# Attention pieces placed in the order of M1 by the planner, and the last bank copied by one instruction

## The chip, the cores and the metric

One Trainium2 chip, one of its cores. The metric is the device time of one execution in microseconds; lower is better. A core has TensorE (PE, with PEld for its weight loads), VectorE (DVE), ScalarE (ACT), GpSimd (POOL) and SyncE (SP), which work at the same time and wait for each other by semaphores. Each takes its own instructions strictly in the order in which the program lists them.

## What is computed

A recurrent attention with a decay (a retention layer), and then a two-layer network with GELU on its output. Per head h the decay is gamma = 1 - 2^(-5-h); inputs q, k, v have shape (4, 8, 768, 64):

```
for t in range(S):
    state = gamma * state + outer(k[t], v[t])
    y[t] = (1 / sqrt(64)) * q[t] @ state
x = y as (batch * 768, 512)
out = gelu_tanh(x @ w_in) @ w_out        # w_in 512x2048, w_out 2048x512
```

The output is 3072 x 512 in float32.

## The kernel before

**Chunks.** The 768 steps are cut into 6 chunks of 128, numbered 0 to 5. A chunk holds 128 steps of all four batches, 512 rows of x. Each chunk passes through three stages.

*Attention of chunk c* consists of TensorE pieces, which the code names and which a line of the profile tells apart: T (L205, 8 transposes that turn q and k of one batch), A (L214, scores of one batch, 16 matmuls of 64x64), yc (L233, what the state gives to y), yi (L245, what the chunk's own scores give to y, 8 matmuls for a batch), and S (L256, the new state; not for the last chunk). Around them stand loads (SP), casts or scalings (ACT, POOL, DVE: L153, L155, L170), the copy of T's output (evT), the multiplication of A's output by a mask on DVE (ev_A1, L265), the write of y as x (ev_Y1, L272), and the update of the state (ev_S2, L277). For chunks 2 to 5 four sums over x follow on POOL (sumx), since M1 needs them.

*M1 of chunk c* is x @ w_in and GELU. For chunk 1 it is 16 plain units of 8 matmuls (L351). For chunks 2 to 5 it is done by a scheme that replaces eight block products by seven with sums of blocks: 4 groups of 7 products (PROD), each of 4 matmuls 128x128x256 (L486). A product adds into one of three banks of PSUM (X, Y, Z); between products the bank is copied out on ACT (snap), added to on DVE (add, L388), and GELU follows on ACT (L367). Products 2 to 6 of a group each need such an eviction of an earlier one; product 0 and 1 need x alone, and the third product of a group, like later ones, needs sums of x.

*M2 of chunk c* is the second layer, for chunk 0 in 16 plain units (L509), and for chunks 1 to 5 in 14 units of 8 matmuls (L498, two for each of the seven products). It needs all of M1 of that chunk and sums over g (sumg, sume on POOL or DVE). The last M2 has nothing beside it.

**What sets the order.** Chunk 0 is written out by hand. For all after it, the code at the end of the function is a planner that runs while the program is built. It holds threads of units for TensorE (thread 0: attention, threads 1 and 2: M1, thread 3: M2) and a list of operations for the other engines, with a cost for each kind (KIND), and buffers and eight PSUM banks as slots. Step by step it finds which engine can start something soonest, and writes that instruction next. A unit of TensorE is taken from the front of a thread; `unit_at` says when its inputs (`needs`) are there, and when the banks that it allocates are free. What is written is a fixed program; the planner's times are its own figures.

Each unit carries a place, the first entry of its tuple. M1 of chunk c has places c + k/28 (chunk 1: c + k/16), M2 of chunk c has c + 1.15 + u/14, and plain M2 of chunk 0 has 0.5 to 0.875. Attention of chunk c is cut into 7 units (chunk 1: 8): T, T, A of batches 0 and 1, T, T, then a unit that takes six banks (yc for two batches, A for two batches, yi for two batches), then yc, yi for the other two batches and S. In the kernel before, these units have places c - 0.9 + 0.01 i. Among the front units that are certain to be ready (`sure`, within 0.03 us), the planner takes attention first whatever its place, and else the one with the lowest place:

```
            h = min(ok, key=lambda h: (h[1] != 0, h[2][0]))
```

And where an attention unit has its inputs but waits for banks, units of M1 that would open a new X bank are held off (`held_off`).

**The last bank.** For the last chunk M2 evicts each bank of 128x256 by itself. The last one of all (product 6, second half of the rows) is copied half by VectorE (L1049) and half by ScalarE (L1050), and then a store on SP (L519) sends it out. Other copies of the kind "snap" go through `copy_on` (L153 on ScalarE).

In the texts below M1(c) is M1 of chunk c, and likewise M2(c). Where the code is reached through a helper, the line is the helper's: L153 is a copy on ScalarE, L388 any tensor_tensor of sums and additions.

Of the kernel before, what the change touches and what calls it, by code (L numbers as in the profile page):

```python
# [16 lines left out]
def kernel(  # L17
# [9 lines left out]
    nc = tc.nc  # L27
# [70 lines left out]
    def load1(eng, nm, c, b):  # L98
# [24 lines left out]
        out=misc[:, 0:1], in_=zero[:, 0:1], func=AF.Gelu_apprx_tanh, scale=1.0  # L123
# [14 lines left out]
    for j in range(2):  # L138
        for hp in range(NHP):
            nc.vector.tensor_scalar(  # L140
                out=mask[:, j, hp],
# [9 lines left out]
    def copy_on(eng, out, in_):  # L151
        if eng is nc.scalar:
            eng.copy(out=out, in_=in_)  # L153
        else:
            eng.tensor_copy(out=out, in_=in_)  # L155
# [46 lines left out]
    def mm_T(c, b, ps):  # L202
        for i, nm in enumerate("qk"):
            for hp in range(NHP):
                nc.tensor.transpose(  # L205
                    out=ps[:, i, hp], in_=pair(h16[nm, c, b], hp), identity=iden
                )
# [56 lines left out]
    def ev_A1(eng, c, b, j, ps):  # L264
        eng.tensor_tensor(out=a_sb[c, b, j], in0=ps, in1=mask[:, j], op=ALU.mult)  # L265
# [115 lines left out]
    hw = d_model // 2  # L381
# [250 lines left out]
    tok, T = {}, {}  # L632
# [17 lines left out]
    def op(*a, **k):  # L650
        todo.append(Op(*a, **k))
# [99 lines left out]
    def att(c):  # L751
        units = []

        def T1(b):
            def emit():
                mm_T(c, b, T["bank", "T", c, b])

            def ev(eng):
                qkT[c, b] = T["qkT", c, b]
                copy_on(eng, qkT[c, b], T["bank", "T", c, b])  # L760

            op("evT", ev, [("T", c, b)], [("qkT", c, b)], alloc=[(("qkT", c, b), 1)],
               free=[("bank", "T", c, b)], slack=0.5)
            return [sub(0.46, emit, [("q16", c, b), ("k16", c, b)], [("T", c, b)],
                        [(("bank", "T", c, b), 1, (128, 2, NHP, 128), F16)],
                        [("qk16", c, b)])]

        def A(b, cost):
            def emit():
                mm_A(c, b, [T["bank", "A", c, b, j] for j in range(2)])  # L770

            for j in range(2):
                r = j ^ b % 2

                def ev(eng, j=j, r=r):
                    a_sb[c, b, j] = T["a", c, b, j]
                    ev_A1(eng, c, b, j, T["bank", "A", c, b, r])

                op("evA", ev, [("A", c, b)], [("a", c, b, j)], alloc=[(("a", c, b, j), 1)],
                   free=[("bank", "A", c, b, r)], slack=1.0)  # L780
            return sub(cost, emit, [("qkT", c, b)], [("A", c, b)],
                       [(("bank", "A", c, b, j), 1) for j in range(2)])

        def yc(bs):
            def emit():
                mm_yc(c, bs, {b: T["bank", "Y", c, b] for b in bs})

            return sub(0.33, emit, [("st", c - 1, b % 2) for b in bs] + [("m1done", c - 2)],
                       [], [(("bank", "Y", c, b), 1) for b in bs], [("qkT", c, b) for b in bs])

        def yi(b, cost):
            def emit():
                mm_yi(c, b, T["bank", "Y", c, b])

            def ev(eng):
                if c not in xT:
                    xT[c] = T["x", c]
                ev_Y1(eng, c, b, T["bank", "Y", c, b])

            op("evY1" if c < 2 else "evY", ev, [("Y", c, b)] + ([("al", "x", c)] if b else []),  # L800
               [("x", c, b)], alloc=[] if b else [(("x", c), 1)],
               early=[] if b else [("al", "x", c)], free=[("bank", "Y", c, b)], slack=0.7)
            return sub(cost, emit, [("a", c, b, j) for j in range(2)] + [("v16", c, b)],
                       [("Y", c, b)], [], [("a", c, b, j) for j in range(2)] + [("v16", c, b)])

        def S(par):
            def emit():
                t = T["bank", "S", c, par]
                for i in range(2):
                    mm_s(c, 2 * i + par, t[:, i])  # L810

            def ev(eng):
                ev_S2(eng, par, T["bank", "S", c, par])

            op("evS", ev, [("S", c, par)], [("st", c, par)], free=[("bank", "S", c, par)], slack=1.5)
            bs = (par, par + 2)
            return sub(0.23, emit, [("k16", c, b) for b in bs] + [("v16", c, b) for b in bs],
                       [("S", c, par)], [(("bank", "S", c, par), 1, (128, 2, NHP, 64))],
                       [(nm, c, b) for b in bs for nm in ("qk16", "v16")])

        units += [T1(0), T1(1)]
        units.append([A(0, 0.35), A(1, 0.33)])
        units += [T1(2), T1(3)]
        if c == 1:
            units += [[yc((0, 1)), yi(0, 0.33), yi(1, 0.33)], [A(2, 0.35), A(3, 0.33)]]
        else:
            units.append([yc((0, 1)), A(2, 0.23), A(3, 0.23), yi(0, 0.33), yi(1, 0.33)])
        units.append([yc((2, 3)), yi(2, 0.33), yi(3, 0.33)] + ([] if c + 1 == NCk else [S(0), S(1)]))
        for j in (1, 3, 2, 4) if c > 1 else ():
            def emit(eng, j=j):  # L830
                xs[c] = T["xs", c]
                sum_of(eng, j, RHS, x_of4(c))

            need = {1: [("x", c, b) for b in range(B)], 3: [("x", c, b) for b in range(B)],
                    2: [("xs", c, 1)], 4: [("xs", c, 2)]}[j]
            op("sumx", emit, need + ([] if j == 1 else [("al", "xs", c)]), [("xs", c, j)],
               alloc=[(("xs", c), 1)] if j == 1 else [], early=[("al", "xs", c)] if j == 1 else [],
               slack=0.6)
        return [(c - 0.9 + 0.01 * i, u, True) for i, u in enumerate(units)]

    def m1_raw(c):
        units = []
# [138 lines left out]
    def m2_w(c):  # L981
        units, last = [], c == NCk - 1
        O = [("o0", c), ("o1", c)]
        for n, (k, lk, rk) in enumerate(PROD):
            for a in range(2):
                key = ("bank", k, c, "m2", a if last else 0)
# [31 lines left out]
                ot = O[at[0]]  # L1018
# [8 lines left out]
                if n in SNAP:  # L1027
                    alloc = [(ot, 1 if not last else 9)] if n in (0, 3) and (not last or a == 0) else []

                    def ev(eng, part=part, ot=ot, bank_of=bank_of):  # L1030
                        copy_on(eng, part(T[ot]), bank_of())

                    op("snap", ev, [did] + ([("al", ot)] if last and a else []), [("ev2", c, n, aa)],
                       alloc=alloc, early=[("al", ot)] if alloc else [], free=[key], slack=0.0)
                elif n in ADD:
                    def ev(eng, part=part, ot=ot, bank_of=bank_of):
                        tt(eng, part(T[ot]), bank_of(), part(T[ot]), ALU.add)

                    op("add", ev, [did, ("ev2", c, SNAP_OF[at], aa)], [("ev2", c, n, aa)],
                       free=[key], slack=0.0)  # L1040
                elif not (last and a == 1):
                    def ev(eng, part=part, ot=ot, bank_of=bank_of):
                        copy_on(eng, part(T[ot]), bank_of())

                    op("snap", ev, [did], [("ev2", c, n, aa)], free=[key], slack=0.2)
                else:
                    def ev(eng, ot=ot, key=key):
                        t, p = T[ot][:, 1], T[key]
                        nc.vector.tensor_copy(out=t[:, 0:hw // 2], in_=p[:, 0:hw // 2])  # L1049
                        nc.scalar.copy(out=t[:, hw // 2:hw], in_=p[:, hw // 2:hw])  # L1050

                    op("snap", ev, [did], [("ev2", c, n, aa)], free=[key], slack=0.2)
                if not last and n > 4:
                    p = n - 5
# [106 lines left out]
    while waiting or any(threads):  # L1161
        best = {}
        fronts, held_off = [], False
        for i, th in enumerate(threads):
# [4 lines left out]
                continue  # L1169
            s = max(need, free_at["PE"], r if r is not None else 1e9)  # L1170
            fronts.append([s, i, th[0], need, r])
        if fronts and fronts[0][1] == 0:
            s, _, _, need, r = fronts[0]
            if need < free_at["PE"] + 0.5 and s > max(need, free_at["PE"]):
                held_off = True
# [3 lines left out]
        fronts = [h for h in fronts if h[0] < 1e8]  # L1179
# [18 lines left out]
        if e == "PE":  # L1198
            sure = min(h[5] for h in fronts)
            ok = [h for h in fronts if h[5] <= sure + 0.03]  # L1200
            h = min(ok, key=lambda h: (h[1] != 0, h[2][0]))
            start_unit(threads[h[1]].pop(0), h[0])
        else:
            ok = [x for x in cand[e] if x[0] <= best[e] + 0.02]
            s, _, o = min(ok, key=lambda x: x[1])
            waiting.remove(o)
            finish_op(o, e, s)
# [30 lines left out]
```

## Time and profile before

| what | value |
|---|---|
| median of 3 runs | 207.44 us (207.22 to 208.33) |
| the profiled execution, its own time | 207.19 us |
| its span, from the first to the last instruction | 205.3 us |
| instructions in the trace | 5809 |
| granted TensorE clock | 1.00 |
| moved by DMA | 30.11 MB |
| last matmul starts | 201.5 us |

A row of TensorE's timeline has its start, its busy time, line, operation, what it writes and reads with shapes, and the count of merged instructions; in brackets stands the idle time before it and what ended that. Matmuls overlap their neighbours by the time in which one still drains, so the distance from one row's start to the next says more than the busy time. Rows of groups have: total busy us, mean ns of one, idle time before them, and what ended it. A row of a window has start:end, length, then busy us of PE, PEld, DVE, ACT and POOL with counts, the granted clock, the DMA share and GB/s.

### The profile page before, as it was taken

The numbers are of one execution on the slowest core, as the hardware profiler recorded it, in microseconds if no ns is written. First come the engines' busy times: TensorE is split into PE (matmuls) and PEld (weight loads), VectorE is DVE, ScalarE is ACT, GpSimd is POOL, SyncE is SP. The second block draws the span as 40 slices with busy tenths as digits, with TensorE's granted clock in tenths as the row PEclk, the third lists the DMA queues.
The fourth block names the chain that finished last, engine by engine and source line by source line (L and its number), as shares of the span: only waits on it lengthen the run. The fifth ranks groups of instructions, "written<-read, shape, count | busy, mean of one in ns | idle before, by whom it ended". The sixth has DMA issues, their size and how long they took to land. (4 is left out here: it accounts for less than half of the span.)

```text
span 205.3 us, 5809 instructions
## 1 busy us (share of the span) xinstructions
PE 196.2 (96%) x2424; PEld 156.6 (76%) x2424; DVE 147.6 (72%) x284; ACT 124.4 (61%) x223; POOL 87.8 (43%) x90
## 2 busy tenths in 40 slices
PE   7869999999999998999999999999999999999993
PEld 2346744455898887788888879888888888888882
DVE  3335585749868999997998899989656864476421
ACT  2482466054689566476599749965856577765311
POOL 0587000030222973936999957982441520024000
PEclk9999999999999999999999999999999999999999
DMA  7999999999998998976799500023000140002204
GB/s 165 287 260 206 209 204 220 219 224 240 247 209 258 255 217 194 264 173 140 231 220 249 126 3 3 0 83 129 0 0 3 42 158 8 0 5 102 102 29 179
DMA packets 83034, 30.11 MB, mean 147 GB/s; under 512 B 75456, under 2 KB 79936, under 8 KB 83008
## 3 DMA queue, kind: packets, MB, share of 16 engines
q1 hardware_dynamic: 72256, 23.45, 45.6%
q0 software_dynamic: 4224, 4.19, 12.3%
q10 hardware_dynamic: 6528, 2.10, 4.1%
q8 instruction: 19, 0.31, 0.6%
q14 instruction: 7, 0.06, 0.1%
HBM read 27.64 MB, written 6.29 MB: 165 GB/s over the span
## 5 line engine op out<-in xcount | busy, mean ns | idle before, releaser
L388 DVE TENSOR_TENSOR st<-ps,st 128x512 f32<-128x512 f32 x48 | 31.7, 683 | 10.1 <-PE ps L486 8.9
L367 ACT ACTIVATE g<-st 128x512 f16<-128x512 f32 x48 | 29.4, 633 | 14.4 <-DVE st L388 14.0
L153 ACT COPY st<-ps 128x512 f32<-128x512 f32 x48 | 27.2, 590 | 11.6 <-PE ps L486 11.4
L498 PEld LDWEIGHTS <-s_g 128*128 128x128 f16 x320 | 31.1, 98 | 3.6
L486 PEld LDWEIGHTS <-w_in 128*128 128x128 f16 x256 | 24.7, 98 | 3.7 <-issue 0.6
L388 POOL TENSOR_TENSOR s_g<-g 128x512 f16<-128x512 f16 x12 | 14.0, 1177 | 30.5 <-ACT st L153 23.4
L351 PEld LDWEIGHTS <-w_in 128*128 128x128 f16 x232 | 20.9, 98 | 7.7 <-issue 0.7
L265 DVE TENSOR_TENSOR a<-ps,mask 128x512 f16<-128x512 f32 x40 | 24.8, 679 | 2.5 <-PE ps L214 2.4
L498 PEld LDWEIGHTS <-g 128*128 128x128 f16 x240 | 23.3, 98 | 2.8
L153 ACT COPY o<-ps 128x512 f32<-128x512 f32 (+1 forms) x27 | 14.3, 528 | 17.7 <-PE ps L498 13.4
L367 ACT ACTIVATE g<-ps 128x512 f16<-128x512 f32 x32 | 19.1, 602 | 7.7 <-PE ps L351 5.2
L486 PEld LDWEIGHTS <-u_w 128*128 128x128 f16 x192 | 18.4, 98 | 2.4
L498 PE MATMUL ps<-w_out,s_g 128*128 128x256 f16 x160 | 19.9, 273 | 0.0
L498 PE MATMUL ps<-t_w,s_g 128*128 128x256 f16 x160 | 19.8, 273 | 0.0
L498 PE MATMUL ps<-w_out,g 128*128 128x256 f16 x160 | 19.8, 273 | 0.0
L388 POOL TENSOR_TENSOR s_g<-g,s_g 128x512 f16<-128x512 f16 x13 | 15.3, 1193 | 10.1 <-ACT g L367 3.9
L486 PE MATMUL ps<-xs,w_in 128*128 128x256 f16 x128 | 19.1, 273 | 0.0
L388 DVE TENSOR_TENSOR s_g<-g 128x512 f16<-128x512 f16 x28 | 14.6, 562 | 6.0 <-ACT g L367 3.6
L388 DVE TENSOR_TENSOR o<-ps,o 128x512 f32<-128x512 f32 (+1 forms) x18 | 10.8, 598 | 11.0 <-PE ps L498 10.9
L486 PE MATMUL ps<-x,w_in 128*128 128x256 f16 x128 | 18.1, 272 | 0.3 <-DVE a L265 0.3
L486 PE MATMUL ps<-xs,u_w 128*128 128x256 f16 x128 | 17.8, 273 | 0.0
L153 ACT COPY qkT<-ps 128x1024 f16<-128x1024 f16 x11 | 11.1, 1018 | 8.2 <-PE ps L205 8.0
(71 smaller groups left out, 319.7 us busy)
## 6 DMA issues: line engine op xcount, KB each, us to landing
ld<-in_k_dram SPq DMA_DIRECT2D x21, 256.0 KB, 4.5
ld<-in_q_dram SPq DMA_DIRECT2D x21, 256.0 KB, 4.4
ld<-in_v_dram SPq DMA_DIRECT2D x19, 256.0 KB, 4.4
out_dram<-o SPq DMA_DIRECT2D x8, 512.0 KB, 2.7
w_in<-in_moe_w_in_dram POOLq DMA_DIRECT2D x4, 512.0 KB, 9.7
w_out<-in_moe_w_out_dram POOLq DMA_DIRECT2D x4, 512.0 KB, 14.7
out_dram<-o SPq DMA_DIRECT2D x5, 256.0 KB, 3.6
st<-in_v_dram SPq DMA_DIRECT2D x3, 256.0 KB, 4.6
```

What stands on the lines that cost most here:

```text
L153: eng.copy(out=out, in_=in_)
L265: eng.tensor_tensor(out=a_sb[c, b, j], in0=ps, in1=mask[:, j], op=ALU.mult)
L351: nc.tensor.matmul(out=out, lhsT=w_in_sb[wi][:, kc, wr * 128:(wr + 1) * 128], rhs=xT[c][:, kc, t0:t1], start=(kc == 0), stop=(kc == NHP - ...
L367: nc.scalar.activation(out=out, in_=in_, func=AF.Gelu_apprx_tanh, scale=1.0)
L388: eng.tensor_tensor(out=out, in0=in0, in1=in1, op=op)
L486: nc.tensor.matmul(out=ps[:, f], lhsT=m1_lhs(lk, kc, 2 * g + f), rhs=x[:, kc], start=(n in FIRST and kc == 0 and f == 0), stop=(n in (1, 5 ...
L498: nc.tensor.matmul(out=ps, lhsT=m2_lhs(c, lk, fp, a), rhs=m2_rhs(rk, fp), start=(first and fp == 0), stop=(n in (1, 5, 6) and fp == NP - 1 ...
```

## The change

The units of attention get places inside the order of M1 of the chunk before: the 7 (or 8) units of chunk c lie evenly from c - 0.7 on over half a chunk. The planner no longer puts thread 0 first: it takes the lowest place among the units that are certain to be ready. Holding M1 off for banks happens only when the attention unit has the lowest place of all front units. And the last bank of the output goes through `copy_on` with the engine that the planner gives to a "snap", which is ScalarE, in one instruction of 128x256 in place of two of 128x128 on VectorE and ScalarE.

```diff
@@ att(c)
-        return [(c - 0.9 + 0.01 * i, u, True) for i, u in enumerate(units)]
+        return [(c - 1 + 0.3 + 0.5 * i / len(units), u, True) for i, u in enumerate(units)]
@@ m2_w(c), the last product of the last chunk
                     def ev(eng, ot=ot, key=key):
-                        t, p = T[ot][:, 1], T[key]
-                        nc.vector.tensor_copy(out=t[:, 0:hw // 2], in_=p[:, 0:hw // 2])
-                        nc.scalar.copy(out=t[:, hw // 2:hw], in_=p[:, hw // 2:hw])
+                        copy_on(eng, T[ot][:, 1, 0:hw], T[key])
@@ the planner's loop
-        if fronts and fronts[0][1] == 0:
+        if fronts and fronts[0][1] == 0 and fronts[0][2][0] <= min(h[2][0] for h in fronts):
             s, _, _, need, r = fronts[0]
             if need < free_at["PE"] + 0.5 and s > max(need, free_at["PE"]):
                 held_off = True
@@
-            h = min(ok, key=lambda h: (h[1] != 0, h[2][0]))
+            h = min(ok, key=lambda h: h[2][0])
             start_unit(threads[h[1]].pop(0), h[0])
```

## The prediction

> **What bounds the kernel now.** I read the page's busy shares and slices first, then the busy time by stage, then TensorE's own timeline (no other engine's) wherever a stage was not full.
>
> ```profile
> PE 196.2 (96%) x2424; PEld 156.6 (76%) x2424; DVE 147.6 (72%) x284; ACT 124.4 (61%) x223; POOL 87.8 (43%) x90
> PE   7869999999999998999999999999999999999993
> ```
>
> TensorE is busy for 96% of the span, and what it lacks lies in the first three slices (the start, which is written out by hand and unchanged) and in the last (the tail). So the planned part, from 34.4 us on, is a TensorE queue with hardly a hole in it. By stage (span, then PE, PEld, DVE, ACT, POOL busy, the granted clock, DMA share and GB/s):
>
> ```profile
> 56.50:88.00 31.50, 30.83 (x466) 26.72 (x461) 28.16 (x56) 21.56 (x38) 18.43 (x18) 1.00 0.98 233
> 88.00:107.00 19.00, 19.00 (x283) 16.61 (x282) 17.71 (x34) 13.66 (x26) 13.70 (x16) 1.00 0.75 188
> 107.00:137.00 30.00, 29.71 (x447) 25.80 (x445) 28.48 (x50) 24.45 (x43) 25.45 (x24) 1.00 0.32 72
> 137.00:164.00 27.00, 27.00 (x323) 23.69 (x322) 19.87 (x37) 16.79 (x33) 10.70 (x10) 1.00 0.12 44
> ```
>
> TensorE lacks 0.67 + 0.29 = 0.96 us here, all of it before 137 us. The modelled ends of matmuls hide part of each hole, so I measure holes by the distance from one piece's start to the next, against the same piece where nothing held it. The free distances:
>
> ```profile
> 101.31 0.64 PE L245 MATMUL ps<-a,v 128*64 128x128 f16 x16
> 101.78 0.67 PE L256 MATMUL ps<-v,qk 128*64 128x64 f16 x32
> 102.38 0.61 PE L486 MATMUL ps<-xs,w_in 128*128 128x256 f16 x4
> 102.83 0.61 PE L205 MATMUL ps<-iden,qk 128*128 128x128 f16 x8
> 103.28 1.04 PE L486 MATMUL ps<-xs,u_w 128*128 128x256 f16 x8
> 104.15 1.04 PE L486 MATMUL ps<-x,w_in 128*128 128x256 f16 x8
> ```
>
> So a pair of yi takes 0.47, the S pair 0.60, an M1 product right after tiled pieces 0.45, one T 0.45 (two 0.90), and eight 128x256 matmuls (two M1 products of 0.44, or one M2 unit) 0.87. The held ones, at four places of the same timeline:
>
> ```profile
> 77.53 0.41 PE L245 MATMUL ps<-a,v 128*64 128x128 f16 x8
> 78.32 0.41 PE L245 MATMUL ps<-a,v 128*64 128x128 f16 x8 [0.38 <-DVE v L170]
> 78.56 0.79 PE L256 MATMUL ps<-v,qk 128*64 128x64 f16 x32
> 79.51 0.61 PE L205 MATMUL ps<-iden,qk 128*128 128x128 f16 x8 [0.15 <-DVE o L388]
> ```
>
> ```profile
> 85.44 1.04 PE L498 MATMUL ps<-w_out,s_g 128*128 128x256 f16 x8
> 86.62 1.20 PE L205 MATMUL ps<-iden,qk 128*128 128x128 f16 x16
> 87.82 0.60 PE L486 MATMUL ps<-xs,u_w 128*128 128x256 f16 x4
> ```
>
> ```profile
> 96.45 0.85 PE L214 MATMUL ps<-qkT 64*64 64x128 f16 x32
> 97.23 0.64 PE L245 MATMUL ps<-a,v 128*64 128x128 f16 x16
> ```
>
> ```profile
> 118.73 0.62 PE L214 MATMUL ps<-qkT 64*64 64x128 f16 x32
> 119.28 0.64 PE L245 MATMUL ps<-a,v 128*64 128x128 f16 x16
> 119.85 0.61 PE L486 MATMUL ps<-xs,w_in 128*128 128x256 f16 x4
> 120.75 1.20 PE L486 MATMUL ps<-x,w_in 128*128 128x256 f16 x8 [0.29 <-DVE a L265]
> 121.78 1.04 PE L498 MATMUL ps<-t_w,s_g 128*128 128x256 f16 x8
> ```
>
> Holes: 77.53 to 78.56 is 1.03 for 0.47 (0.56); then 0.95 for 0.60 (0.35); 85.44 to 86.62 is 1.18 for 0.87 (0.31); 86.62 to 87.82, two T, is 1.20 for 0.90 (0.30); 96.45 to 97.23 is 0.78, where the same piece at 118.73 took 0.55 (0.23); 119.85 to 120.75 is 0.90 for 0.45 (0.45); then 1.03 for 0.87 (0.16). Together 2.36 us. All stand at or beside attention pieces, and in the stages where VectorE is 89 to 95% busy. After 121.8 us nothing is held (the stage 137 to 164 is busy for 27.00 of 27.00), and the attention of chunk 5 runs there without a hole, from this row on:
>
> ```profile
> 125.49 0.61 PE L205 MATMUL ps<-iden,qk 128*128 128x128 f16 x8
> ```
>
>
> **Part 1: the order.** No matmul, copy or load is added or removed; TensorE's work is the same, so the change can win at most the 2.36 us of holes and can lose only by new ones. The planner compares places. M1 of chunk c has c to c+0.96 (steps of 1/28, for chunk 1 of 1/16), M2 of chunk c has c+1.15 to c+2.08 (steps of 1/14), and attention of chunk c gets c-0.70 to c-0.27 in 7 steps (8 for chunk 1). Before, attention went first whenever it was ready; now it goes when no ready unit has a lower place. I counted the products in TensorE's rows (4 matmuls each, 28 a chunk) to see what is displaced.
>
> - Chunk 1 (41 to 56 us): its places 0.30 to 0.74 lie under those of the M2 units they compete with (0.70 and up when the first T is ready). Nothing changes.
> - Chunk 2 (57 to 79 us): T, A and yi move by one M1 unit (0.87 us) at most. The last piece waits for v (the row at 78.32), and when it is ready every other place is above it, as before. I leave the first two holes, 0.91 us, where they are.
> - Chunk 3 (79 to 102 us): the first two T stay; T 2 and 3, then the six-bank unit (yc, A, yi) at 2.66, let M1 products with lower places pass, so they come some units later.
> - Chunk 4 moves from 102.83 (M1(2) at product 23) to M1(3) product 9, some 12 us later. Chunk 5 moves from 125.49 to M1(4) product 9, some 22 us later, and its last piece to about 158 us.
>
> With a piece go its evictions, its casts, and its loads through SP's queue, since a load waits for a cast to free its buffer. Loads that end at 118 us now will end some 20 us later, among stores that stand behind them on SP; DMA is at 0.32 and 0.12 of its time there, so I cost this at nothing, and a store that had to wait would cost about one load's 1.15 us (the planner's own figure in finish_op), which I leave to the range.
>
> What the move does to VectorE: a chunk's attention is 8 mask multiplications, 4 x evictions and (but for chunk 5) 8 state updates.
>
> ```profile
> L265 DVE TENSOR_TENSOR a<-ps,mask 128x512 f16<-128x512 f32 x40 | 24.8, 679 | 2.5 <-PE ps L214 2.4
> L272 DVE TENSOR_TENSOR x<-ps,dec 128x512 f16<-128x512 f32 x16 | 10.3, 675 | 0.0
> ```
>
> 8 x 0.679 + 4 x 0.675 = 8.1 us. About half of chunk 5's leaves the stage 107 to 137 (28.5 busy of 30.0, so 24.4) for the stage 137 to 164 (19.9 of 27.0, so 24). Both are then about as free as the stage in which chunk 5 ran without a hole. Hence the holes from 85 us on, 0.31 + 0.30 + 0.23 + 0.45 + 0.16 = 1.45 us, can go, all or none; new ones can arise to about the same size. I take half of them gone on balance, 0.7 us, between the chunk that shows none and the chunks that show 0.5 to 0.9 each.
>
> **Part 2: the tail.**
>
> ```profile
> 200.95 0.37 ACT L153 COPY o<-ps 128x256 f32<-128x256 f32 x1 [4.00 <-PE ps L498]
> ```
>
> ```profile
> 201.82 0.29 DVE L1049 COPY o<-ps 128x128 f32<-128x128 f32 x1 [1.32 <-PE ps L498]
> 202.15 0.27 ACT L1050 COPY o<-ps 128x128 f32<-128x128 f32 x1 [0.83 <-DVE o L1049]
> 202.44 0.33 SPq L519 DMA_DIRECT2D out_dram<-o  x1
> ```
>
> The two halves run one after the other: ScalarE starts 0.33 after VectorE, and the store goes 0.62 after the first copy starts. One ScalarE copy of the whole bank is the first row, 0.37, so the store goes 0.39 after: 0.23 us less, all on the path, with nothing beside it. The bounds are 0 (a ScalarE wake-up as long as the saving) and 0.25.
>
> The Trainium skill, "PSUM — Partial Sum Buffer", Specifications (TRN2), says that ScalarE and VectorE read PSUM in parallel at full bandwidth as long as they don't collide on a bank; were these halves parallel, they would end after 0.29, and one copy of 0.37 would be 0.08 slower. The halves lie in one bank, and the trace has them in series, so the proviso decides, not the rule.
>
> **The sum.** The profiled execution took 207.19 us (span 205.3 and 1.9 around it). 207.19 - 0.23 - 0.70 = 206.26. The median of the three runs is 207.44, 0.25 above it, so I expect a median of 206.5; since a re-planned queue also makes a hole or two that no row here can show, I round up to **206.6 us**, 0.4% below. A measurement of this kernel tells about 0.5% (1.04 us) from no change.
>
> **The rivals.**
>
> *All holes from 85 us on go, and those at 77 us too.* For it: chunk 5 without a hole. Against it: the v of chunk 2 is late by its load. 207.44 - 0.23 - 1.45 = 205.76, and with all 2.36 us, 204.85.
>
> *The order hardly takes effect*, because readiness (banks, loads) and not the place decides. For it: chunks 1 and 2. Against: chunks 4 and 5 have nothing that holds them back. Then only the tail counts: 207.2.
>
> *M1 runs bare (slower).* Attention of chunk c+1 ends nearer to M1(c+1), which from its third product on needs the sums of x. From the last piece (c+0.73) to that product stand 7 products and 3 M2 units, then one M2 unit and two products: 9 x 0.44 + 4 x 0.87 = 7.4 us, and 0.6 more where S follows. In chunk 3 now, yi ends at 101.78 (a row above). The first of these rows ends the sum of x that the second needs:
>
> ```profile
> 106.61 1.16 POOL L388 TENSOR_TENSOR xs<-x,xs 128x512 f16<-128x512 f16 x1
> ```
>
> ```profile
> 108.33 0.60 PE L486 MATMUL ps<-xs,u_w 128*128 128x256 f16 x4
> ```
>
> 107.77 - 101.78 = 6.0 us. So it decides from sums that come 1.4 us later than these. Then M2(c) fills TensorE and is missing beside M1(c+1), which alone is bound by ScalarE:
>
> ```profile
> L367 ACT ACTIVATE g<-st 128x512 f16<-128x512 f32 x48 | 29.4, 633 | 14.4 <-DVE st L388 14.0
> L153 ACT COPY st<-ps 128x512 f32<-128x512 f32 x48 | 27.2, 590 | 11.6 <-PE ps L486 11.4
> ```
>
> A group of 7 products takes 3.06 us on TensorE, but 3 x 0.590 + 4 x 0.633 = 4.30 on ScalarE: 1.24 us for each bare group. In M1(5) nothing follows to even it out. One group gives 207.2 + 1.24 = 208.4, two 209.7, all four 212.2. Against it: chunk 3 has the shortest such distance now, and shows no hole at 108.33.
>
> What could make the sums late is seen here:
>
> ```profile
> 117.83 2.26 DVE L170 TENSOR_TENSOR v<-ld,cst 128x512 f16<-128x512 f32 x2
> 118.06 2.94 POOL L170 TENSOR_TENSOR v<-ld,cst 128x512 f16<-128x512 f32 x2
> ```
>
> Run together, they take 1.13 and 1.47 each, where a sum on POOL has 1.16; four sums slowed so are 1.2 us late, just under the 1.4. The Trainium skill, "SBUF — State Buffer", Who interferes with whom, says that VectorE with two SBUF inputs and GpSimd reading SBUF lock each other out of a shared port for a whole instruction; by it four waits could pass 1.4 us, and this rival would be the forecast; the row shows a slowing and not a full block.
>
> **How the numbers follow.** Forecast (206.0 to 207.0) 0.42, of which 0.08 falls below 206.4; all holes go (204.85 to 206.0) 0.27; no effect (207.2) 0.10; bare M1 (208.4 to 212.2) 0.21, of which 0.02 would be offset to within 0.5%. Faster 0.27 + 0.08 = 0.35; same 0.34 + 0.10 + 0.02 = 0.46; slower 0.19. The range goes from 205.0, near the second case's end, to 209.2, between one and two bare groups: about 0.02 lies below and 0.10 above. The likeliest case alone has 206.0 to 207.0.
>
> **What would show it.** Right: chunk 5's first T (L205, the last four pieces) near 147 us and its last yi near 158; stage 107 to 137 with VectorE near 24 us; 16-matmul yi at 0.47 and no bracket at TensorE's rows after 85 us; one ScalarE copy of 0.37 before the last store. Wrong: the same pieces at the same times as now; or M1(5) products with brackets naming ScalarE or POOL, and M2(4) finished several units before M1(5). I would be wrong altogether if readiness beyond 57 us shifts the plan early, by other loads or banks, since every later place rests on it.

## The result, and the profile after

Before takes 207.18 us (median of 7 runs, 206.84 to 208.33), after 205.53 us (median of 7, 205.35 to 206.19). The ratio of after to before is 0.9922, with a 95% interval of 0.9899 to 0.9946. The changed kernel is 0.8% faster, where 0.4% was forecast. Its profiled execution took 205.87 us, with a span of 204.1.

The page of after, busy shares and TensorE's slices, read first as before:

```profile
PE 194.9 (96%) x2424; PEld 156.0 (76%) x2424; DVE 144.1 (71%) x278; ACT 124.4 (61%) x226; POOL 94.0 (46%) x92
PE   7669999999999998999999999999999999999993
```

The shares hardly differ: 2424 matmuls both times, 96% both times. What changed is seen only by stage. Columns as in the prediction (start:end, length, then busy us of PE, PEld, DVE, ACT, POOL, the clock, DMA):

```profile
56.50:88.00 31.50, 30.85 (x472) 26.80 (x465) 28.86 (x57) 21.69 (x40) 17.27 (x16) 1.00 0.96 229
107.00:137.00 30.00, 30.00 (x419) 26.43 (x418) 23.79 (x43) 22.56 (x42) 23.86 (x23) 1.00 0.49 124
137.00:164.00 27.00, 27.00 (x341) 23.91 (x340) 21.11 (x44) 19.65 (x36) 9.51 (x10) 1.00 0.11 40
164.00:189.40 25.40, 25.40 (x258) 22.44 (x257) 16.28 (x30) 17.60 (x32) 13.56 (x12) 1.00 0.06 23
```

The stage 107 to 137 is now full on TensorE (29.71 before), with VectorE down from 28.48 to 23.79. The stage 56.5 to 88 is as it was. There, TensorE's own timeline:

```profile
77.70 0.41 PE L245 MATMUL ps<-a,v 128*64 128x128 f16 x8
78.48 0.41 PE L245 MATMUL ps<-a,v 128*64 128x128 f16 x8 [0.37 <-DVE v L170]
78.73 0.80 PE L256 MATMUL ps<-v,qk 128*64 128x64 f16 x32
79.68 0.61 PE L205 MATMUL ps<-iden,qk 128*128 128x128 f16 x8 [0.15 <-DVE o L388]
...
85.61 1.04 PE L498 MATMUL ps<-w_out,s_g 128*128 128x256 f16 x8
86.78 0.49 PE L486 MATMUL ps<-xs,u_w 128*128 128x256 f16 x3
```

Measured from start to start against the free distances of the prediction, three holes are left, each 0.17 us later than its twin of before: 1.03 for 0.47 (0.56), 0.95 for 0.60 (0.35), 1.17 for 0.87 (0.30). The holes at 86.62 (0.30), 96.45 (0.23), 119.85 and 120.75 (0.61 together) have no successor, and no new one stands anywhere after 57 us. At the end, the last copy in the timeline of all engines:

```profile
200.83 0.37 ACT L153 COPY o<-ps 128x256 f32<-128x256 f32 x1 [0.50 <-PE ps L498]
```

One copy of 0.37 stands in place of the two that took 0.62 in series.

**Where the time went.** I add one measure, the length of the planned part: from the first plain M2 unit (L509) to the start of the last matmul. It is 167.13 us before and 165.96 after, 1.17 less, and the holes are 2.38 and 1.20, 1.18 less. From the last matmul's start to the span's end it is 3.79 and 3.57, 0.23 less before rounding. The planned part starts 0.17 later in the profiled execution of after, and 0.10 less lies around the span. 1.17 + 0.23 - 0.17 + 0.10 = 1.33 us; the two profiled executions differ by 1.32. The medians differ by 1.65. The remaining 0.33 is within the scatter of the start, which lies between 33.94 and 34.6 us in 12 of the 14 profiled executions, with the same code; that it is this scatter was not shown.

### The profile page after: what moved, and what is told of

Read it like the earlier page. It is cut to its first block, busy times and chain, and to the rows that moved or that the text cites. A ratio compares the mean times of both kernels' runs of the same rounds, so it can differ in the third digit from the quotient of the medians.

```text
span 204.1 us, 5789 instructions
## 1 busy us (share of the span) xinstructions
PE 194.9 (96%) x2424; PEld 156.0 (76%) x2424; DVE 144.1 (71%) x278; ACT 124.4 (61%) x226; POOL 94.0 (46%) x92
## 4 chain that ended last, share of the span: by engine, by line
PE 84%; DVE 5%; DMA 5%; ACT 3%; POOL 1%; ACTq 1%; issue 0%
PE ps L498 26%; PE ps L486 23%; PE ps L351 7%; PE ps L509 7%; PE h_ps L351 7%; PE ps L205 4%; DMA st<-in_k_dram 3%; PE ps L245 3%; PE ps L214 2%; DMA ld<-in_k_dram 2%; PE ps L233 2%; PE spin_ps L129 1%; DVE v L170 1%; DVE st L277 1%; ACT qkT L153 1%; ACT g L367 1%
## 5 line engine op out<-in xcount | busy, mean ns | idle before, releaser
L388 DVE TENSOR_TENSOR st<-ps,st 128x512 f32<-128x512 f32 x48 | 31.3, 684 | 14.2 <-PE ps L486 10.3
L367 ACT ACTIVATE g<-st 128x512 f16<-128x512 f32 x48 | 30.0, 636 | 11.7 <-DVE st L388 11.4
L388 POOL TENSOR_TENSOR s_g<-g 128x512 f16<-128x512 f16 x19 | 22.2, 1186 | 20.8 <-PE ps L498 12.0
L153 ACT COPY o<-ps 128x512 f32<-128x512 f32 (+1 forms) x28 | 14.7, 525 | 27.2 <-PE ps L498 22.3
L153 ACT COPY st<-ps 128x512 f32<-128x512 f32 x48 | 26.3, 598 | 5.5 <-PE ps L486 5.5
L498 PE MATMUL ps<-t_w,s_g 128*128 128x256 f16 x160 | 18.9, 273 | 0.0
L388 POOL TENSOR_TENSOR s_g<-s_g,g 128x512 f16<-128x512 f16 x11 | 13.4, 1214 | 10.1 <-DVE s_g L388 10.0
L388 POOL TENSOR_TENSOR s_g<-g,s_g 128x512 f16<-128x512 f16 x11 | 13.0, 1191 | 10.1 <-DVE s_g L388 5.9
L486 PE MATMUL ps<-xs,u_w 128*128 128x256 f16 x128 | 16.6, 273 | 0.1
L486 PE MATMUL ps<-x,w_in 128*128 128x256 f16 x128 | 16.6, 273 | 0.0
L388 DVE TENSOR_TENSOR o<-ps,o 128x512 f32<-128x512 f32 (+1 forms) x18 | 10.8, 599 | 7.6 <-PE ps L498 6.4
L170 POOL TENSOR_TENSOR v<-ld,cst 128x512 f16<-128x512 f32 x10 | 11.2, 1130 | 10.7 <-DMA ld<-in_v_dram 10.7
```

Of the source, the lines that this page charges most:

```text
L170: eng.tensor_tensor(out=o, in0=heads(src, sw), in1=heads(cst[:, col:col + H].unsqueeze(2), sw).broadcast_to([128, NHP, 2, Dh]), op=ALU.mult,)
L367: nc.scalar.activation(out=out, in_=in_, func=AF.Gelu_apprx_tanh, scale=1.0)
L388: eng.tensor_tensor(out=out, in0=in0, in1=in1, op=op)
L486: nc.tensor.matmul(out=ps[:, f], lhsT=m1_lhs(lk, kc, 2 * g + f), rhs=x[:, kc], start=(n in FIRST and kc == 0 and f == 0), stop=(n in (1, 5 ...
L498: nc.tensor.matmul(out=ps, lhsT=m2_lhs(c, lk, fp, a), rhs=m2_rhs(rk, fp), start=(first and fp == 0), stop=(n in (1, 5, 6) and fp == NP - 1 ...
```

## The experiments

**What had to be told apart.** *Theory A*, the prediction's: the attention of chunks 3 to 5 crowded VectorE in 85 to 121 us, TensorE waited there, and spreading it took those holes away. *Rival B*: the old order was an unlucky one, and nearly any other would do. *Rival C*: most of the gain is the tail. For the three holes that stay there were two more: *the port*, by which single VectorE instructions stand still beside GpSimd right ahead of something that TensorE needs, and *the load*, by which v of chunk 2 comes late (the prediction's reason).

All runs in one table. "Holes" are those of TensorE after 57 us in the profiled execution; "length" is that of the planned part. Each ratio is against executions of before that were run alongside, whose medians were 207.04 to 207.18 us, so the ratios compare better across rows than the medians do.

| kernel | median us | ratio to before (95%) | holes us | length us |
|---|---|---|---|---|
| before | 207.18 | 1 | 2.38 | 167.13 |
| after | 205.53 | 0.9922 (0.9899 to 0.9946) | 1.20 | 165.96 |
| order_only | 205.78 | 0.9950 (0.9925 to 0.9975) | 1.22 | 165.98 |
| tail_only | 206.86 | 0.9989 (0.9965 to 1.0013) | 2.39 | 167.14 |
| old_places | 209.20 | 1.0105 (1.0073 to 1.0137) | 4.64 | 169.49 |
| late_places | 207.95 | 1.0040 (1.0013 to 1.0067) | 3.58 | 168.38 |
| old_hold | 207.43 | 1.0013 (0.9991 to 1.0034) | 2.97 | 167.75 |
| before_scale_later | 207.57 | 1.0018 (0.9988 to 1.0048) | 2.62 | 167.37 |
| after_scale_first | 205.76 | 0.9939 (0.9913 to 0.9966) | 1.46 | 166.22 |
| after_scale_later | 205.08 | 0.9900 (0.9865 to 0.9936) | 0.91 | 165.68 |
| after_both | 205.44 | 0.9924 (0.9895 to 0.9954) | 0.92 | 165.69 |
| sums_on_vector | 204.43 | 0.9889 (0.9857 to 0.9922) | 0 | 164.83 |
| sums_and_scale | 204.95 | 0.9901 (0.9866 to 0.9936) | 0 | 164.78 |
| sums_planned | 211.49 | 1.0193 (1.0159 to 1.0228) | 8.05 | 172.91 |

In every row the length less the holes is between 164.7 and 164.9 us (the 8.05 of sums_planned hold 2.9 us of slowed matmuls, of which more below). So TensorE's work in the planned part is a constant, and an order is worth just the holes that it makes.

### The two parts alone

order_only is after with the old two half copies at the end. tail_only is before with the one copy:

```diff
@@ tail_only
-                        nc.vector.tensor_copy(out=t[:, 0:hw // 2], in_=p[:, 0:hw // 2])
-                        nc.scalar.copy(out=t[:, hw // 2:hw], in_=p[:, hw // 2:hw])
+                        copy_on(eng, T[ot][:, 1, 0:hw], T[key])
```

> The changed order with the old last copies (two halves on two engines). Theory (three holes of TensorE go, 0.30 + 0.23 + 0.61 = 1.14 us): ratio to the kernel before about 0.9945, TensorE's order and holes as in the changed kernel, the last store 0.62 after the first copy starts. Rival (the single copy is worth more than the 0.23 us of its rows, since the measured gain of 1.65 us is more than 1.14 + 0.23): ratio 0.997 or above.

> The order of before with the one last copy. Theory: the store goes 0.39 us after the last matmul, not 0.62, so 0.2 us less: ratio 0.9989, all holes of before in place. Rival (the tail is worth the rest of the gain, 0.5 us): ratio 0.9975. A ratio of 1.000 would say that the store waits for something else.

The order alone gives 0.9950, the tail alone 0.9989, whose interval includes no change. In the trace the tail is clearer: from the last matmul's start to the span's end 3.56 us in tail_only, 3.80 in order_only, 3.79 and 3.57 in before and after. So the copy brings 0.23 us and the order the rest, and rival C falls.

### The rule without the places, the places later, and the old hold

Each is after with one line changed: the old places (old_places), places half a chunk before the chunk's start at the earliest (late_places), and the old condition for holding M1 off (old_hold).

```diff
@@ old_places
-        return [(c - 1 + 0.3 + 0.5 * i / len(units), u, True) for i, u in enumerate(units)]
+        return [(c - 0.9 + 0.01 * i, u, True) for i, u in enumerate(units)]
@@ late_places
+        return [(c - 1 + 0.5 + 0.5 * i / len(units), u, True) for i, u in enumerate(units)]
@@ old_hold
-        if fronts and fronts[0][1] == 0 and fronts[0][2][0] <= min(h[2][0] for h in fronts):
+        if fronts and fronts[0][1] == 0:
```

> The changed rule (lowest place first, no preference for attention) and the one copy, but with attention's old places c - 0.9 + 0.01 i, so that it is early and yet not ahead of the first products of the M1 before. The prediction's reason (attention has to leave the crowded stretch 107 to 137 us of VectorE): part of it leaves only, holes of 0.5 to 1.1 us stay beyond 86 us, ratio 0.996 to 0.999. Rival (any other order avoids them, since they hang on single meetings of VectorE and GpSimd): ratio 0.993 as with the new places.

> The changed kernel with attention 0.2 of a chunk later: places c - 0.5 to c - 0.07. From the last piece to the first product that needs the sums of x then stand 7.4 - 0.2 x 29 = 1.6 us of other work in the order of places, where the chain took 6.0 us, so M1 is 4.4 us late at each of three boundaries. If M1 then runs bare and is bound by ScalarE, as the prediction's slower rival has it, 1.24 us for each bare group: 207 to 210 us. If the planner's fill with M2 costs nothing, as it seems at 169 to 172 us of the changed kernel: 205.5.

> The changed kernel with the old condition for holding M1 off: for any attention unit that waits for banks, whatever its place. The planner's own list has 3.2 us of waits of TensorE after 57 us, at the ends of M1 and the starts of M2. If these are what a run shows: ratio to before 1.008. If the new places alone make the gain: 0.992.

All three lose the gain, so rival B falls: another order is not a better one by itself. old_places is slower than either of its expectations had it. Where they lose differs. TensorE's timeline of old_places:

```profile
103.13 1.04 PE L486 MATMUL ps<-xs,u_w 128*128 128x256 f16 x8
104.70 0.60 PE L486 MATMUL ps<-xs,w_in 128*128 128x256 f16 x4 [0.53 <-DVE st L388]
...
140.04 1.04 PE L486 MATMUL ps<-xs,u_w 128*128 128x256 f16 x8
141.80 1.03 PE L486 MATMUL ps<-xs,u_w 128*128 128x256 f16 x8 [0.73 <-ACT st L153]
```

From 103.13 to 104.70 are 1.57 us for 0.87, from 140.04 to 141.80 1.76 for 0.87. M1 products follow M1 products, and TensorE waits for the additions (L388, three waits) and one copy (L153) of the banks that it has just filled. This is the prediction's "M1 runs bare", in another place than was feared and mostly for VectorE, where the prediction priced ScalarE, at 0.5 to 0.9 us a time. By the order of the rows it happens where attention has been spent early and M2 is not at hand; that was not tried by itself.

late_places loses only in chunk 2 (74.89 to 80.8 us) and has no hole after it:

```profile
74.89 0.41 PE L245 MATMUL ps<-a,v 128*64 128x128 f16 x8
76.98 0.41 PE L245 MATMUL ps<-a,v 128*64 128x128 f16 x8 [1.67 <-DVE v L170]
```

From 74.89 to 76.98 are 2.09 us for half a pair of yi, 0.23: a hole of 1.86. It is not the pair of 77.70 of after, which is that of the last two batches: here the second yi of the six-bank unit, batch 1, waits for its v. VectorE's timeline of late_places:

```profile
71.80 3.23 DVE L388 TENSOR_TENSOR s_g<-g 128x512 f16<-128x512 f16 x4
74.95 1.37 DVE L388 TENSOR_TENSOR s_g<-s_g,g 128x512 f16<-128x512 f16 x1
76.24 0.68 DVE L170 TENSOR_TENSOR v<-ld,cst 128x512 f16<-128x512 f32 x1
```

The scaling at 76.24 stands behind sums that take 3.23 for four and 1.37 for one, where such a sum takes 0.41 with GpSimd idle (a row further below). For chunks 3 to 5 these later places are as good as those of the change. And old_hold has one large hole late, in M2, next to small ones at 135.56 and 138.12:

```profile
169.34 0.82 PE L498 MATMUL ps<-t_w,s_g 128*128 128x256 f16 x6
171.30 0.94 PE L498 MATMUL ps<-t_w,s_g 128*128 128x256 f16 x7 [1.14 <-DVE s_g L388]
```

M2 waits there for a sum over g on VectorE, and that sum (at 169.88), too, takes 1.37. So neither the new rule with the old places nor the new places with the old hold brings the gain. The new places with the old rule, attention first, were not run.

### Moving one scaling in VectorE's queue

In these kernels the planner's lists for all other engines stay; only the position of a few instructions in VectorE's list is moved, by holding them back until another has been written. The keys name what an operation gives.

```diff
-        o.emit(ENG[e])
+        mine = next((r for k, r in HOLD.items() if k in o.gives), None)
+        if mine:
+            held_emits.setdefault(mine, []).append((o, e))
+        else:
+            o.emit(ENG[e])
+        for n in o.gives:
+            for o2, e2 in held_emits.pop(n, []):
+                o2.emit(ENG[e2])
@@ before_scale_later (on before): two scalings of v go behind the mask multiplication
+    HOLD = {("v16", 5, 0): ("a", 4, 3, 1), ("v16", 5, 1): ("a", 4, 3, 1)}
@@ after_scale_first (on after): two sums go behind, so v of chunk 2 is scaled sooner
+    HOLD = {("sw", 3, 3): ("ev2", 1, 1, 1), ("gs", 1, 4, 1): ("ev2", 1, 1, 1)}
@@ after_scale_later (on after): a scaling of v for chunk 3 goes behind a mask multiplication
+    HOLD = {("v16", 3, 0): ("a", 3, 1, 1)}
@@ after_both: the last two together
```

> The kernel before with the same order of every engine, but two scalings of v of chunk 5 (VectorE, 117.83 us, 2.26 us for both beside GpSimd) stand behind the four mask multiplications that they stood ahead of. VectorE has the same work in the same stretch. Lock theory (a hole of TensorE comes where a VectorE instruction with two operands in SBUF stands still until a GpSimd instruction ends, ahead of an eviction whose bank TensorE needs): the two holes at 119.85 and 120.75 (0.45 + 0.16) go, the rest stays, ratio 0.997. Fullness theory of the prediction (VectorE is too full in this stage): holes of about the same sum come back a few us later, ratio 1.000.

> The changed kernel with the same order of every engine, but on VectorE at 76.7 us a sum of w_in and a sum of g go behind the scaling of v of chunk 2, batch 3, and the two additions after it. Its load landed at 62 us. Lock theory: v is scaled by 77.8 instead of 78.4, the additions free their banks 0.6 earlier, and the holes at 77.70 and 78.73 (0.56 + 0.35) shrink to 0.1 to 0.3 together: 0.6 to 0.8 us less than the changed kernel, ratio to before 0.989. Load theory of the prediction (v is late by its load): nothing changes, ratio 0.992.

> The changed kernel with the same order of every engine, but the scaling of v of chunk 3, batch 0 (VectorE, 84.49 us, 1.64 us beside GpSimd, against 0.68 alone) goes behind the four mask multiplications after it. Lock theory: the multiplications start 1.5 us earlier and the hole at 85.61 (0.29) goes: ratio to before 0.991. If the hole had another cause (its row names none), it stays: 0.992.

> Both moves of after_scale_first and after_scale_later on the changed kernel. Lock theory: 0.9 to 1.1 us less than the changed kernel, about 204.6 us, ratio to before 0.987, and no hole over 0.2 us left from 57 us to the last matmul. Fullness or load theory: 205.5 us.

Each move does what it says where it is made. In before_scale_later the holes at 119.85 and 120.75 are gone, so the two scalings at 117.83 had made them. In after_scale_first the hole of 0.56 is gone, so v of chunk 2 was not late by its load: the same scaling ran 1.6 us earlier. VectorE's timeline of after_scale_first (in after, the scaling stands at 77.75):

```profile
76.17 1.04 DVE L170 TENSOR_TENSOR v<-ld,cst 128x512 f16<-128x512 f32 x1
```

But the time comes back elsewhere. TensorE's timeline of after_scale_first, then that of before_scale_later:

```profile
83.84 0.42 PE L214 MATMUL ps<-qkT 64*64 64x128 f16 x16 [0.49 <-DVE qkT L155]
...
86.48 0.60 PE L486 MATMUL ps<-xs,u_w 128*128 128x256 f16 x4 [0.37 <-DVE a L265]
```

```profile
124.14 0.44 PE L256 MATMUL ps<-v,qk 128*64 128x64 f16 x16 [0.15 <-DVE st L388]
...
141.06 0.60 PE L486 MATMUL ps<-xs,u_w 128*128 128x256 f16 x4 [0.21 <-ACT o L153]
```

after_scale_first wins 0.67 and loses 0.93 (0.68 at 82.94, 0.25 more at 85.07); before_scale_later wins 0.61 and loses 0.87. Only after_scale_later wins outright, the 0.29 at 85.6; its lead on after is within the intervals. after_both, for which up to 1.1 us were expected, keeps the new 0.68 of after_scale_first (at 83.53) and is no better than after_scale_later. So the port, as a matter of one instruction ahead of one bank, fails: in a stretch where VectorE is hardly ever idle (17.70 of 18.00 us from 70 to 88 us, a row below) a different order hands the lateness to another instruction. What had to be asked is why VectorE is so full there.

### Taking GpSimd's work away from beside VectorE

VectorE's timeline of after around the holes, and GpSimd's:

```profile
72.85 3.35 DVE L388 TENSOR_TENSOR s_g<-g 128x512 f16<-128x512 f16 x4 [0.30 <-ACT g L367]
...
76.72 0.77 DVE L388 TENSOR_TENSOR w_in<-w_in 128x512 f16<-128x512 f16 x1
77.41 0.41 DVE L388 TENSOR_TENSOR s_g<-g,s_g 128x512 f16<-128x512 f16 x1
77.75 0.68 DVE L170 TENSOR_TENSOR v<-ld,cst 128x512 f16<-128x512 f32 x1
...
84.49 1.64 DVE L170 TENSOR_TENSOR v<-ld,cst 128x512 f16<-128x512 f32 x1
```

```profile
75.88 1.33 POOL L388 TENSOR_TENSOR s_g<-s_g,g 128x512 f16<-128x512 f16 x1
79.22 0.61 POOL L155 CAST qk<-ld 128x512 f16<-128x512 f32 x1 [2.01 <-PE ps L256]
...
83.13 2.44 POOL L388 TENSOR_TENSOR xs<-x,xs 128x512 f16<-128x512 f16 x2
```

The rows to compare are those of one operation. With GpSimd idle from 77.21 to 79.22, a sum takes 0.41 (at 77.41) and a scaling 0.68 (at 77.75). The sum at 76.72 takes 0.77: GpSimd's sum of 75.88 ends at 77.21, and this one ends 0.28 later. The scaling at 84.49 takes 1.64: GpSimd's pair ends at 85.57, and it ends 0.56 later. Neither shares data with the GpSimd instruction beside it (the first adds blocks of weights). So a VectorE instruction with both operands in SBUF that starts while one of GpSimd runs stands still until GpSimd's ends. These are no chosen pairs: in all fourteen traces after 57 us, 175 sums of 128x512 started so, and all but 10 ended 0.28 us after GpSimd's instruction, within 0.02 (in the 10, GpSimd's ended within 0.1 us of the sum's start, and the sum took 0.41 to 0.43); 40 scalings ended 0.55 to 0.58 after it. Whichever engine comes second waits: 71 sums that were already running when GpSimd's started took 0.41 to 0.42. And an instruction that reads PSUM isn't held (the addition of 76.12 takes 0.68 beside the same sum of GpSimd). The Trainium skill, "SBUF — State Buffer", Who interferes with whom, says this: VectorE with two SBUF inputs and GpSimd reading SBUF exclude each other for a whole instruction. These rows agree.

sums_on_vector puts three of GpSimd's sums over g, those at 73.36 to 77.21, on VectorE, in the same place of the same list:

```diff
-        o.emit(ENG[e])
+        o.emit(ENG[{("gs",1,2,3): "DVE", ("gs",1,4,3): "DVE", ("gs",1,2,2): "DVE"}.get(o.gives[0] if o.gives else None, e)])
```

sums_and_scale adds the HOLD of after_scale_later.

> The changed kernel with the same order, but the three sums of g that GpSimd runs from 73.4 to 77.2 us run on VectorE, at their place in the list. VectorE gets 3 x 0.35 us more work, and no GpSimd instruction is beside its sums from 72 to 77 us, where they stood still for 0.96 + 0.95 + 0.35 us. Lock theory (what fills VectorE here is standing still for GpSimd): VectorE is 1.2 us ahead by 78 us, the holes at 77.70 and 78.73 (0.91) go to 0.2 or less, ratio to before 0.988. Fullness without a lock (VectorE simply has too much work): 1.05 us more work makes the holes larger, ratio 0.994 to 0.997.

> sums_on_vector, and the scaling of v of chunk 3 behind the four mask multiplications as in after_scale_later. Lock theory: all three holes after 57 us (1.20) go but for 0.2: 1.0 us less than the changed kernel, ratio to before 0.987. If holes here only move within VectorE's full stretch, as in after_scale_first: 0.991 to 0.993.

The stretch from 70 to 88 us, in after and then in sums_on_vector (columns as above):

```profile
70.00:88.00 18.00, 17.35 (x240) 14.97 (x239) 17.70 (x33) 10.74 (x21) 13.34 (x13) 1.00 0.93 211
```

```profile
70.00:88.00 18.00, 18.00 (x255) 15.86 (x253) 17.60 (x37) 12.02 (x22) 10.54 (x11) 1.00 0.98 222
```

VectorE does 37 instructions in the time of 33, and TensorE is full. VectorE's and TensorE's timelines of sums_on_vector:

```profile
72.24 1.43 DVE L388 TENSOR_TENSOR s_g<-g 128x512 f16<-128x512 f16 x4 [0.30 <-ACT g L367]
...
75.20 0.69 DVE L170 TENSOR_TENSOR v<-ld,cst 128x512 f16<-128x512 f32 x1
```

```profile
77.09 0.64 PE L245 MATMUL ps<-a,v 128*64 128x128 f16 x16
77.57 0.67 PE L256 MATMUL ps<-v,qk 128*64 128x64 f16 x32
78.17 0.62 PE L205 MATMUL ps<-iden,qk 128*128 128x128 f16 x8
```

Four sums take 1.43 instead of 3.35, v is scaled 2.55 us earlier, and the pair of yi, S and T follow at 0.48 and 0.60, the free distances. All three holes are gone, at 85 us too, and the length is 164.83. So a part of VectorE's fullness there was standing still, and more work on VectorE was less time: over single rows of 57 to 88 us, sums and scalings stood still for 3.7 us in after and for 1.5 here. VectorE is as full as before (17.60 of 18.00), with more done. At 204.43 us, 0.9889 of before, this is the best kernel of the study. Against after its interval overlaps; the holes say that it is 1.2 us shorter. sums_and_scale has no hole to take away any more, and gives the same within its interval.

### Letting the planner do it

sums_planned puts all sums over g of chunk 1 on VectorE by their kind, and lets the planner arrange the rest, with v's scalings more urgent (due 2 us after they can start, in place of 8):

```diff
+        "sumd": {"DVE": (0.35, 0.42)},
-            slack=8.0 if nm == "v" else 2.0,
+            slack=2.0 if nm == "v" else 2.0,
-                op("sumg" if c + 1 < NCk else "sume", emit, need, [("gs", c, j, g)], slack=3.0 if g < 3 else 1.0)
+                op(("sumd" if c == 1 else "sumg") if c + 1 < NCk else "sume", emit, need, [("gs", c, j, g)], slack=3.0 if g < 3 else 1.0)
```

> The changed kernel, with the planner told to give all sums of g of chunk 1 to VectorE, and the scalings of v a nearer due time (2 in place of 8 us). The planner's own list then has 0.08 us of waits of TensorE after 57 us, where it has 0.31 for the changed kernel and 1.56 for the one before. If the planner's list is a guide: ratio to before 0.986 to 0.989. If meetings of VectorE and GpSimd elsewhere make new holes: 0.990 to 0.995.

It is the slowest kernel of all, against both expectations (0.986 to 0.995). The profiled execution, 213.58 us, took longer than its other five (210.01 to 212.04), so its rows tell the mechanism and not the median. VectorE's timeline, GpSimd's, then TensorE's stages and timeline:

```profile
82.83 2.44 DVE L388 TENSOR_TENSOR s_g<-g 128x512 f16<-128x512 f16 x2
85.20 1.26 DVE L388 TENSOR_TENSOR w_in<-w_in 128x512 f16<-128x512 f16 x1
```

```profile
81.42 4.76 POOL L170 TENSOR_TENSOR v<-ld,cst 128x512 f16<-128x512 f32 x4
```

```profile
83.00:88.00 5.00, 1.10 (x11) 0.74 (x8) 5.00 (x6) 0.20 (x1) 4.48 (x5) 0.94 0.97 220
88.00:94.00 6.00, 5.69 (x27) 4.06 (x28) 4.02 (x9) 4.54 (x8) 0.00 (x0) 0.50 0.95 214
```

```profile
88.31 1.04 PE L486 MATMUL ps<-xs,w_in 128*128 128x256 f16 x4 [4.21 <-DVE st L388]
89.14 1.91 PE L486 MATMUL ps<-x,w_in 128*128 128x256 f16 x8
90.84 1.06 PE L486 MATMUL ps<-xs,w_in 128*128 128x256 f16 x4
```

The planner now has scalings of v on GpSimd, back to back, beside a row of sums on VectorE. Each sum stands still for one scaling (1.2 us in place of 0.42), and the additions to M1's banks stand behind them. That is not for want of the rule in the planner. Its code, in all these kernels, lets what uses the shared port start one after the other:

```python
    def shared(o, e):
        return e == "POOL" or e == "DVE" and o.kind[:3] in ("sum", "sca")
    ...
        if shared(o, e):
            port[0] = s + busy
    ...
                s = max(free_at[e], n, r, port[0] if shared(o, e) else 0.0)
```

By the planner's own times GpSimd waits for a row of seven sums on VectorE, 7 x 0.35 = 2.45 us. But these times are a reckoning; what is written for VectorE and for GpSimd are two lists, and nothing in the code shown makes GpSimd wait for VectorE's row. In the trace GpSimd's sum of x (78.79), two casts and the scalings run in between, and the seven sums take from 78.84 to 86.46, 7.6 us. So the list looked good to itself (0.08 us of waits). TensorE waits 4.21 us. Near the end of the wait the granted clock falls to 0.50 (its mean is 0.94 from 83 to 88 us and 0.50 from 88 to 94), and about 6 us of work run at that clock: eight matmuls from 89.14 on take 1.70 in place of 0.87. The pieces from 88.31 to 94.3 lose 2.9 us in this way, beside the 4.4 of the wait. How much is lost differs by execution: the mean clock of this one is 0.976, that of the other five 0.984 or 0.992.

## Why the prediction was right, and where it was not

**Bound.** Right. The gain is holes of TensorE in the planned part, as the constant of the table shows in all orders, and the tail.

**Part 2.** Right: 0.23 forecast, 0.23 between the two traces and 0.23 between tail_only and before. What puts the two halves in series is seen as a wait: the bracket of ScalarE's half names VectorE's copy. Whether it stands there for the bank or for the output tile, no run tells.

**Part 1, the size.** The term that was mis-sized is "half of them gone on balance, 0.7 us": 1.18 us went. Of the 1.45 from 85 us on only the 0.30 at 85.44 stayed, and no new hole came. Rounding up by a tenth or so "since a re-planned queue also makes a hole or two" was wrong for this order, though not for its neighbours: old_places, late_places and old_hold make 0.6 to 2.3 us more holes than before. With 1.18 in place of 0.70, the working gives 207.19 - 0.23 - 1.18 = 205.78 for the profiled execution, which took 205.87. So the outcome is less the forecast than its rival "all holes from 85 us on go": the measured 205.53 lies in that case's 204.85 to 206.0 (chance 0.27) and outside the 206.0 to 207.0 of the likeliest case (0.42). The sign, the tail and the place of the holes that went were right; how many went was not, and the time was inside the range because the range took in most of that rival's case.

**The two holes of chunk 2.** They stayed as forecast, for another reason. "The v of chunk 2 is late by its load" fails: after_scale_first and sums_on_vector scale it 1.6 and 2.55 us earlier. It stands in VectorE's queue behind sums that stand still.

**The positions.** Wrong in both directions. TensorE's timeline of after:

```profile
138.91 0.61 PE L205 MATMUL ps<-iden,qk 128*128 128x128 f16 x8
...
165.11 0.64 PE L245 MATMUL ps<-a,v 128*64 128x128 f16 x16
...
168.31 1.04 PE L498 MATMUL ps<-w_out,g 128*128 128x256 f16 x8
169.19 3.66 PE L498 MATMUL ps<-t_w,s_g 128*128 128x256 f16 x32
172.68 1.58 PE L486 MATMUL ps<-xs,u_w 128*128 128x256 f16 x13
```

Chunk 5's first T came at 138.91 (forecast 147), its last yi at 165.11 (forecast 158). I counted places and forgot that a unit which isn't ready doesn't compete. By the rows, T pieces are taken early while M1 waits for the sums of x, and the six-bank unit, which needs six free banks, comes only behind the last products of M1 of the chunk before; that it is the banks was read from the order and not tried by itself. So, by these rows, attention lies now in the stretches where M1 has little to give TensorE, at both ends of a chunk. The load on VectorE came out near the forecast in 107 to 137 (24.4 forecast, 23.79) and under it in 137 to 164 (24 forecast, 21.11), where part of it has slipped past 164.

**The rival "M1 runs bare".** Its sign showed: five units of M2(4) run ahead (168.31 to 172.68) while M1(5) waits. It cost nothing, with TensorE at 25.40 of 25.40 from 164 to 189.4. As a mechanism it is real: old_places has it at 0.5 to 0.9 us a place, less than the 1.24 reckoned for a group and mostly as waits for VectorE.

**The port.** "The row shows a slowing and not a full block" was a misreading of merged rows. Two rows with x2 show a mean; single rows set against the other engine's end show the block. The planner's code has the block as a rule, too (`shared`, `port`). By the block, this rival would have been the forecast, and the change came out faster all the same; but the block explains the 1.2 us of holes that the change left.

**Open.** What made the holes at 86.62 and 96.45 was not tried by itself, nor was GpSimd freed of sums in the other chunks, or put in turn with VectorE by semaphores. So it is not settled why the change takes holes away. The rows of before point at the same standing still. The single rows behind the merged pair of the prediction, VectorE's and GpSimd's:

```profile
118.57 1.52 DVE L170 TENSOR_TENSOR v<-ld,cst 128x512 f16<-128x512 f32 x1
```

```profile
118.06 1.49 POOL L170 TENSOR_TENSOR v<-ld,cst 128x512 f16<-128x512 f32 x1
```

VectorE's scaling ends 0.54 after GpSimd's, and the mask multiplications for which TensorE waits at 120.75 stand behind it. Ahead of the hole at 96.45 a sum takes 1.37 (at 94.26), ahead of 86.62 a scaling 1.64 (at 84.33). Added up over single rows, VectorE stands still for 3.0 us in 107 to 137 us of before and for 1.5 in after, so about a third of the 4.7 us by which it is less busy there is standing still, and the rest is work moved away. The 1.5 us left make no hole. Which of the two, less work or fewer meetings, takes the holes away, no run separates.

## What to carry to other kernels

Where one engine is full and its work is fixed, measure every order by the same two numbers, the length of the full part and the sum of its holes; if the difference is a constant, as it was here, an order is worth its holes and no more. Where reordering a queue only moved a hole, as here, the engine behind it was full, and the question was what its instructions stood still for. A planner that reckons with a resource that two engines share, but doesn't write their turns into the program, can make its best list the slowest kernel.

## What the runs showed of the hardware that I had not expected

- VectorE beside GpSimd isn't done when the GpSimd instruction ends: the sum ends 0.28 us later, the scaling with a float32 input 0.56 later (of 0.41 and 0.68 when free). Standing still of this kind adds up to 9.1 us of VectorE's time from 57 us on in before, 6.4 in after and 4.1 in sums_on_vector, by single rows set against the free ones. And moving work from the idler engine to the fuller one saved time.
- In the profiled execution of sums_planned a wait of 4.21 us by TensorE goes with about 6 us of work at a granted clock of 0.50, so there the wait costs two thirds more than its length (2.9 on 4.4). The longest of the shorter holes, 1.86 us in late_places, left the clock at 1.00 (72 to 82 us). The Trainium skill, "TensorE: Matmul & The Clock Gate", Part 1, says that the clock is halved after an idle window of about 3.4 us and comes back after as long a busy one; the wait of 4.21 agrees, and the way back took about 6 us, more than one such window.
